# Forward bursts of batches 1 to 7 further apart, inverse bursts later, and the second layer of tile 2 as a direct product

## The chip, the cores and the metric

The kernel runs on one core of a Trainium2 chip. The metric is the time of one execution on the device, in microseconds (us). "Before" stands for the kernel as it was, "after" for the kernel with the change. The engines are called PE (TensorE's matmuls), PEld (its weight loads), DVE (VectorE), ACT (ScalarE), POOL (GpSimd) and SP (SyncE, which here only issues DMAs). L468 is line 468 of the kernel before.

## The reference

The input x has 8 batches of 3008 rows and 256 columns. Each column is filtered along its batch's rows in the frequency domain, and the result goes, row by row, through two dense layers with a Gelu between them.

```python
X = np.fft.rfft(x, axis=1)                       # x: 8 x 3008 x 256
y = np.fft.irfft(X * (filt_r + 1j * filt_i), n=3008, axis=1)
h = y.reshape(24064, 256) @ w_in                 # w_in: 256 x 2048
g = 0.5 * h * (1.0 + erf(h / sqrt(2)))
out = g @ w_out                                  # w_out: 2048 x 256
```

## The kernel before

**The filter.** 3008 is 47 x 64, and the transform is done as matmuls in stages. For batches 1 to 7 the stages are these. `fold` adds and subtracts halves of x on DVE, in place (L107, L108). `s1` (L430) multiplies by the first table; its result a_sb is stored to a DRAM tile R1 by SP (L439) and read back with another layout as b_sb by `r1` (L445). `s2` (L457) is the forward burst: 32 small matmuls into four PSUM banks. `s2_out` (L468) multiplies one of these four banks by the filter on DVE. On every second call it also combines the real and imaginary parts of a pair, by L471 and L472. `s3` (L485) is the inverse burst of the same unit: 32 small matmuls that read p, the result of `s2_out`. ACT copies it to v_sb, SP stores that to a DRAM tile R2 (L495), and `r2` (L503) reads it back as d_sb. `s4` (L512) finishes the inverse transform with four matmuls a call, and ACT or DVE writes the result into a ring y_sb. Each batch has three units u = 0, 1, 2 of `s2`, `s2_out`, `s3`, and b_sb has two buffers, so that the third `r1` follows the first unit's burst. Batch 0 goes another way, ahead of the main loop.

**The layers.** The 24064 rows are 47 tiles of 512. `mm1` (L637) makes one sixteenth of a tile's hidden layer by two matmuls of 512 columns (four where the tile wraps around the ring), and ACT applies Gelu (L640) into g_sb. The second layer of a tile is done, for all tiles but tile 0, by `mm2_seven` (L709): the 2 x 2 block product is made by seven products instead of eight, each in 16 matmuls of 128 columns, so 112 in all. It needs sums of quarters of g_sb, made on DVE by `sums_1` (L678, four calls a tile), `sums_2` (L684, two) and `sums_3` (L691, two). DVE also evacuates the products from PSUM and adds them up in eight operations a tile (L724 to L738). The products use two PSUM banks of the kind `o` in turn, a new one from products 0, 1, 3 and 5 on: L724 frees the first, L726 and L729 the second, L731 to L735 the third, the two of L738 the last. Tile 0 is done directly, by `mm2_first` (L650): 64 matmuls of 256 columns, and two copies from PSUM on DVE.

**The order.** Nothing is ordered by the machine. The main loop goes over slots s; slot s belongs to tile t = s // 16 and place jc = s % 16. In each slot the kernel first issues what a table `at` holds for this slot, then a sixteenth of the second layer of tile t - 1, then a sixteenth of the first layer of tile t:

```python
for f, a in at.pop(s, ()):
    f(*a)
...
if t - 1 in seven:
    ...
    m.mm2_seven(t - 1, n(jc), n(jc + 1))
```

So every engine's queue is in this order, and each engine works through its queue without passing anything by. The table is filled by hand-written formulas. `first(b)`, called `hi`, is the first slot of the tile in which batch b's rows begin: 80, 176, 272, 368, 464, 560 and 656 for batches 1 to 7. `sums_1` of a tile stand at places 12, 13 and 15 of its own tile and 1 of the next, `sums_2` at 0 and 1 of the next, `sums_3` at 5 and 8. `s1` of batches 3 to 6 stands at `hi - 94` to `hi - 83`, the first two `r1` at `hi - 80`. The slots of `s2` are the table `s2` in the code, and `s2_out`, `s3`, the third `r1`, the first `r2` (after[b]) and the loads of the next batch's x (`load_next`, on POOL, behind a small copy that waits for p) hang on them. `s4` is placed backwards from the slot in which its rows are needed, and goes out of the way of slots that are marked busy, which are those around bursts.

PSUM has three banks of the kind `h`, two `o` and three `f`. `s2` and `s3` take one `h` and three `f`; `s1` and `s4` use `f` too.

Of the kernel before, what the change touches and what calls it, by code (L numbers as in the profile page):

```python
# [10 lines left out]
ALU = mybir.AluOpType  # L11
# [11 lines left out]
TCH = 512  # L23
# [8 lines left out]
class _Mix:  # L32
# [428 lines left out]
    def s2_out(self, b, u, m, d):  # L461

        if d == 0:
            self.st[b, "p", 2 * u + m] = self.pp.tile([128, 2, 2, 2, 256], BF16, tag="p12", name="p12")
        w, a, v = self.st[b, "p", 2 * u + m], m ^ d, self.nc.vector.tensor_tensor
        ps = self.st[b, "ps2"][m][d].rearrange("p (r c) -> p r c", r=2)
        f = self.Fu[:, :, a, 2 * u + m, :]
        v(out=w[:, a], in0=ps.unsqueeze(2).to_broadcast([128, 2, 2, 256]),  # L468
          in1=f.unsqueeze(1).to_broadcast([128, 2, 2, 256]), op=ALU.mult)
        if d:  # L470
            v(out=w[:, :, 0, 0], in0=w[:, :, 0, 0], in1=w[:, :, 1, 1], op=ALU.subtract)  # L471
            v(out=w[:, :, 0, 1], in0=w[:, :, 0, 1], in1=w[:, :, 1, 0], op=ALU.add)  # L472

    def s3(self, b, u):

# [163 lines left out]
            o += n  # L639
        nc.scalar.activation(out=self.st["g", t][:, jc, :], in_=ps, func=AF.Gelu)  # L640

    def mm2_first(self, lo, hi):

        nc = self.nc
        for n in range(lo, hi):
            jc, q = (n // 2, n % 2) if n < 32 else (n % 16, n // 16)
            if n < 2:
                self.st["o2", q] = self.bank("ps_o", "o").rearrange("p (a b) -> p a b", a=2)
            ps = self.st["o2", q % 2]
            nc.tensor.matmul(ps[:, q // 2, :], lhsT=self.st["g", 0][:, jc, q * 128:q * 128 + 128],  # L650
                             rhs=self.w_out_sb[:, jc, :], start=(jc == 0), stop=(jc == 15))
            if q > 1 and jc == 15:
                ost = self.po.tile([128, 2, 256], FP32, tag="ost", name="ost")
                nc.vector.tensor_copy(out=ost, in_=ps)
                for a in range(2):
                    self.put_rows((q - 2 + 2 * a) * 128, ost[:, a], nc.sync)

    def weight_sums(self):

# [33 lines left out]
    def mm2_seven(self, t, lo, hi):  # L693

        nc, v = self.nc, self.nc.vector.tensor_tensor
        a11, a12, s2, a22 = self.quarters(t)
        w = self.w_out_sb.rearrange("p (i k) (n o) -> p k n i o", k=2, n=2)
        q = self.w_sums
        s31, s4 = self.st["s", t], self.st.get(("s4", t))
        ops = ((a11, w[:, 0, 0]), (a12, w[:, 1, 0]), (s2, q[:, 1]), (s31[:, :, 0], q[:, 2]),  # L700
               (s31[:, :, 1], q[:, 0]), (a22, q[:, 3]), (s4, w[:, 1, 1]))
        last = t == self.B * self.S // TCH - 1
        for n in range(lo, hi):
            m, sub, i = n // 16, n // 8 % 2, n % 8
            if n % 16 == 0 and (m == 0 or m % 2 == 1) or last and m > 4 and i == 0:
                self.st["o"] = self.bank("ps_o", "h" if n > 80 else "o").rearrange("p (m s o) -> p m s o", m=2, s=2)
            ps = self.st["o"]
            a, b = ops[m]
            nc.tensor.matmul(ps[:, (m + 1) % 2, sub, :], lhsT=a[:, i, 128 * sub:128 * sub + 128], rhs=b[:, i],  # L709
                             start=i == 0, stop=i == 7)  # L710
            if last and m > 4 and i == 7:
                self.finish(t, m, sub, ps)
            if n % 16 != 15 or m % 2 or last and m > 4:
                continue
            p0, p1 = ps[:, 0], ps[:, 1]
            if m == 0:
                self.st["t"] = self.po.tile([128, 2, 2, 128], FP32, tag="ost", name="t_sb")
                self.st["c"] = [None, None]
            if m in (2, 4):
                self.st["c"][m // 4] = self.po.tile([128, 2, 256], FP32, tag="ost", name="ost")  # L720
            t1, t3 = self.st["t"][:, 0], self.st["t"][:, 1]
            c = lambda h, k: self.st["c"][h][:, :, 128 * k:128 * k + 128]
            if m == 0:
                nc.vector.tensor_copy(out=t1, in_=p1)  # L724
            elif m == 2:
                v(out=c(0, 0), in0=t1, in1=p0, op=ALU.add)  # L726
                if last:
                    self.store(t, 0, 0, nc.sync)
                v(out=t1, in0=t1, in1=p1, op=ALU.add)  # L729
            elif m == 4:  # L730
                v(out=t3, in0=t1, in1=p0, op=ALU.subtract)  # L731
                v(out=c(1, 1), in0=t3, in1=p1, op=ALU.add)
                if last:
                    self.store(t, 1, 1, nc.scalar)
                v(out=t1, in0=t1, in1=p1, op=ALU.add)  # L735
            else:
                for h, tt, p in ((1, t3, p0), (0, t1, p1)):
                    v(out=c(h, 1 - h), in0=tt, in1=p, op=ALU.add)  # L738
                    for sub in range(2):
                        self.put_rows(t * TCH + 256 * h + 128 * sub, self.st["c"][h][:, sub],  # L740
                                      nc.gpsimd if t > 1 or h > sub else nc.sync)

    def put_rows(self, r0, tile_, eng):

# [33 lines left out]
def kernel(  # L778
# [9 lines left out]
    m = _Mix(ctx, tc, x, filt_r, filt_i, moe_w_in, moe_w_out, out)  # L788
    nc, B, S = tc.nc, m.B, m.S
    NT = B * S // TCH  # L790
    ctx.enter_context(tc.manual_schedule())

    g = m.small
# [112 lines left out]
    def put(slot, f, *a):  # L906
        at.setdefault(slot, []).append((f, a))

    def first(b):
        return (b * S // TCH) * 16  # L910

    busy, crowd, after = set(), set(), {}
    for b in range(1, B):
        hi = first(b)
        e = 4 * (b == B - 1)
        s1, n1, r1 = (4, 2.75, 16) if b == 1 else (hi - 87, 3.7, hi - 73) if b == 2 else (hi - 94 - e, 3.7, hi - 80 - e)
        s2 = (33, 45, 57) if b == 1 else (hi - 64 - 2 * e + (b == 2), hi - 48 - 3 * e + e // 4, hi - 32 - 3 * e)
        busy.update(range(s1 - 1, s1 + int(3 * n1) + 2))
        for c in range(4):
            slot = s1 + int(c * n1 + (b == 1 and c in (1, 2)))  # L920
            put((0, 1, 5, 8)[c] if b == 1 else (67, 69, 86, 94)[c] if b == 2 else s1 - 28 + e + 6 * c, m.fold, b, c)
            put(slot, m.s1, b, c)
        for u in range(3):
            put(r1 if u < 2 else s2[0] + 1, m.r1, b, u)
            put(s2[u], m.s2, b, u)
            for i in range(4):
                put(s2[u] + ((0, 2, 5, 6)[i] if b == u == 1 else 2 * i + (b == 2 and u == 0)), m.s2_out, b, u, i // 2, i % 2)
            s3 = s2[u] + (9 if b == 1 and u != 1 else 10)
            put(s3, m.s3, b, u)
            put(s3 + 1, m.s3_out, b, u, 1)  # L930
            busy.update(range(s2[u] - 1, s2[u] + 5), range(s3 - 1, s3 + 2))
        after[b] = s3 + (5 if b > 1 else 4)
        crowd.update(range(s2[0], after[b]), range(s1 + 66, s1 + 94))
        if b + 1 < B:
            for i, (u, o, p) in enumerate(((0, 5, 1), (0, 7, 1), (1, 1, 2), (1, 5, 3), (1, 7, 3), (2, 1, 4), (2, 5, 5), (2, 7, 5))):
                put(s2[u] + o, m.load_next, b, p, i // 2, i % 2)
# [34 lines left out]
    put(1, m.load_filters_again, nc.gpsimd, 0, 2)  # L971
    put(18, m.load_filters_again, nc.sync, 2, 4)
    put(20, m.weight_sums)
    seven = range(1, NT)
    for t in seven:
        for i, s in enumerate((12, 13, 15, 16 if t == S // TCH - 1 else 17)):
            put(16 * t + s, m.sums_1, t, 2 * i)
# [5 lines left out]
    for s in range((NT + 1) * 16):  # L983
        t, jc = s // 16, s % 16
        for f, a in at.pop(s, ()):
            f(*a)
        pace = lambda i: max(16 * (i - 6) // 10, 0) if t == late else i
        if t - 1 in seven:
            n = lambda i: (14 * i if i < 6 else 84 + 28 * (i - 6) // 10) if t == late else 7 * i
            m.mm2_seven(t - 1, n(jc), n(jc + 1))  # L990
        elif t < 2:
            n = lambda i: max(4 * i - 40, 0) if i < 16 else min(24 + 8 * (i - 16) // 3, 64)
            m.mm2_first(n(s), n(s + 1))
        for i in range(pace(jc), pace(jc + 1)) if t < NT else ():
            m.mm1(t, i)
    assert not at
# [30 lines left out]
```

## Time and profile before

| What | Value |
|---|---|
| Time, median of 3 runs (lowest to highest) | 751.08 us (750.72 to 751.89) |
| Time of the profiled execution | 750.39 us |
| Its span | 748.6 us |
| PE busy | 730.8 us, 9261 matmuls |
| DVE busy | 616.9 us, 1120 instructions |
| ACT busy | 575.1 us, 1048 instructions |
| POOL busy | 288.2 us, 544 instructions |
| Granted clock of PE | 1.00 |
| Sums and evacuations a tile on DVE | 4 of L678 at 687 ns, 2 of L684 at 707, 2 of L691 at 693, 8 evacuations at 413 to 421 |
| A unit on DVE | 4 of L468 at 1217 ns, 2 each of L471 and L472 at 432 and 436 |

The span goes from the first to the last instruction of the profiled execution; the time of the execution has 1.8 us around it. An instruction on DVE shows its whole duration, and the next may start a little before its end, so lengths of a queue are counted from start to start. Ends of matmuls are modelled, so PE's own waits are also read from start to start. A line of a timeline gives start and duration in us, engine, line and operation, what it writes and reads, how many instructions are merged, and in brackets the idle time before it and what ended that.

### The profile page before, as it was taken

To read this page: it belongs to the slowest core of one execution; us is meant where nothing else is said; L and a number is where in the kernel's file an instruction comes from. 1 tells how busy PE (TensorE), PEld (TensorE's weight loads), DVE (VectorE), ACT (ScalarE), POOL (GpSimd) and SP (SyncE) were. 2 spreads that over 40 slices of the span, in tenths; PEclk is the share of its full clock that TensorE was granted. 3 is DMA by queue.
4 is the path that set the end of the run, shared out by engine and by line. 5 is a ranking of instruction groups with operands and counts; after the bars stand their busy time and mean duration, and the time that the engine had idled before them with its cause. 6 is when DMAs were issued, how large, how long until landed. Compare 5 with 4: busy or idle time off the path is not lost.

```text
span 748.6 us, 22400 instructions
## 1 busy us (share of the span) xinstructions
PE 730.8 (98%) x9261; PEld 508.9 (68%) x9261; DVE 616.9 (82%) x1120; ACT 575.1 (77%) x1048; POOL 288.2 (39%) x544
## 2 busy tenths in 40 slices
PE   8999999999999999999999999999999999999997
PEld 4856666666777667666677666666767766777776
DVE  8977998899887998789977989769997898676566
ACT  6987777677887788878887777877878787777773
POOL 7893446666122552234431355114631122112121
PEclk9999999999999999999999999999999999999999
DMA  9996542745345552546535455355444433301011
GB/s 154 213 193 185 125 109 86 212 90 123 86 121 177 117 119 82 142 148 134 112 103 162 111 126 131 90 158 129 117 108 118 153 91 99 117 31 58 29 57 58
DMA packets 81353, 89.31 MB, mean 119 GB/s; under 512 B 13171, under 2 KB 60659, under 8 KB 81251
## 3 DMA queue, kind: packets, MB, share of 16 engines
q0 software_dynamic: 22352, 39.76, 23.1%
q1 hardware_dynamic: 58483, 47.93, 22.8%
q8 instruction: 72, 1.18, 0.7%
q14 instruction: 30, 0.25, 0.1%
q10 hardware_dynamic: 416, 0.20, 0.1%
HBM read 55.57 MB, written 48.23 MB: 139 GB/s over the span
## 4 chain that ended last, share of the span: by engine, by line
PE 77%; DVE 15%; DMA 3%; POOL 2%; issue 2%; ACT 0%; DVEq 0%; POOLq 0%; SPq 0%
PE ps_h L637 35%; PE ps_o L709 33%; DVE p L468 5%; DMA x_sb<-in_x_dram 3%; PE ps_s L512 2%; PE ps_s L430 2%; DVE s_sb L678 2%; POOL out_dram L756 1%; PE ps_s L485 1%; DVE p L472 1%; PE ps_s L457 1%; DVE g_sb L684 1%; PE ps_o L650 1%; DVE s_sb L691 1%; DVE x_sb L108 1%
## 5 line engine op out<-in xcount | busy, mean ns | idle before, releaser
L640 ACT ACTIVATE g_sb<-ps_h 128x512 f16<-128x512 f32 x752 | 447.9, 603 | 146.1 <-PE ps_h L637 142.5
L637 PE MATMUL ps_h<-y_sb,w_in_sb 128*128 128x512 bf16 (+3 forms) x1600 | 445.3, 366 | 0.2 <-DVE a_sb L328 0.2
L756 POOL DMA_DIRECT2D out_dram<-ost x228 | 129.4, 574 | 389.3 <-DVE ost L738 359.4
L709 PEld LDWEIGHTS <-g_sb 128*128 128x128 f16 x2944 | 193.9, 98 | 90.1 <-issue 13.5
L709 PEld LDWEIGHTS <-s_sb 128*128 128x128 f16 x2208 | 147.8, 98 | 56.7 <-issue 3.7
L709 PE MATMUL ps_o<-w_sums,g_sb 128*128 128x128 f16 x1472 | 127.5, 219 | 4.7 <-DVE t_sb L729 3.5
L637 PEld LDWEIGHTS <-w_in_sb 128*128 128x128 bf16 x1600 | 125.0, 98 | 8.5 <-issue 1.1
L709 PE MATMUL ps_o<-w_sums,s_sb 128*128 128x128 f16 x1472 | 126.2, 219 | 0.1
L709 PE MATMUL ps_o<-w_out_sb,g_sb 128*128 128x128 f16 x1472 | 119.4, 219 | 2.1 <-DVE ost L738 2.1
L678 DVE TENSOR_TENSOR s_sb<-g_sb 128x1024 f16<-128x1024 f16 x184 | 120.3, 687 | 0.8 <-ACT g_sb L640 0.8
L468 DVE TENSOR_TENSOR p<-ps_s,F 128x1024 bf16<-128x1024 f32 x84 | 102.1, 1217 | 3.5 <-PE ps_s L457 1.8
L99 POOL DMA_DIRECT2D x_sb<-in_x_dram x156 | 79.0, 513 | 2.4 <-DMA x_sb<-in_x_dram 0.8
L684 DVE TENSOR_TENSOR g_sb<-s_sb,g_sb 128x1024 f16<-128x1024 f16 x92 | 65.0, 707 | 1.6
L709 PE MATMUL ps_o<-w_out_sb,s_sb 128*128 128x128 f16 x736 | 63.9, 219 | 0.0
L691 DVE TENSOR_TENSOR s_sb<-g_sb 128x1024 f16<-128x1024 f16 x92 | 63.8, 693 | 0.0
L731 DVE TENSOR_TENSOR t_sb<-t_sb,ps_o 128x256 f32<-128x256 f32 x46 | 19.3, 419 | 40.9 <-PE ps_o L709 39.7
L326 ACT ACTIVATE v_sb<-ps_s 128x512 bf16<-128x512 f32 x83 | 45.5, 608 | 6.3 <-PE ps_s L485 5.7
L326 ACT ACTIVATE y_sb<-ps_s 128x376 bf16<-128x376 f32 x94 | 46.6, 496 | 4.6 <-PE ps_s L512 4.6
L512 PEld LDWEIGHTS <-d_sb 96*128 96x128 bf16 x448 | 31.2, 97 | 27.2 <-issue 2.2
L738 DVE TENSOR_TENSOR ost<-t_sb,ps_o 128x256 f32<-128x256 f32 x90 | 33.7, 415 | 18.1 <-PE ps_o L709 18.1
L328 DVE CAST a_sb<-ps_s 128x512 bf16<-128x512 f32 x54 | 34.7, 684 | 12.7 <-PE ps_s L430 12.4
L726 DVE TENSOR_TENSOR ost<-t_sb,ps_o 128x256 f32<-128x256 f32 x46 | 19.1, 416 | 24.7 <-PE ps_o L709 24.1
(156 smaller groups left out, 556.7 us busy)
## 6 DMA issues: line engine op xcount, KB each, us to landing
out_dram<-ost POOLq DMA_DIRECT2D x126, 128.0 KB, 2.7
b_sb<-R SPq DMA_DIRECT2D x21, 512.0 KB, 5.2
R<-v_sb SPq DMA_DIRECT2D x84, 128.0 KB, 2.6
d_sb<-R SPq DMA_DIRECT2D x56, 192.0 KB, 3.3
R<-a_sb SPq DMA_DIRECT2D x108, 96.0 KB, 2.2
x_sb<-in_x_dram POOLq DMA_DIRECT2D x48, 94.0 KB, 2.7
x_sb<-in_x_dram POOLq DMA_DIRECT2D x48, 48.0 KB, 2.7
x_sb<-in_x_dram POOLq DMA_DIRECT2D x12, 188.0 KB, 5.1
```

Of the source, the lines that this page charges most:

```text
L99: self.nc.gpsimd.dma_start(out=xt[64 * v + to:64 * v + to + m, h, 4 * c:4 * c + 4 * n, :], in_=xv[h][at:at + m, w:w + 4 * n, :])
L326: self.nc.scalar.activation(out=out, in_=in_, func=AF.Copy, scale=1.0 if scale is None else scale)
L328: self.nc.vector.tensor_copy(out=out, in_=in_)
L468: v(out=w[:, a], in0=ps.unsqueeze(2).to_broadcast([128, 2, 2, 256]), in1=f.unsqueeze(1).to_broadcast([128, 2, 2, 256]), op=ALU.mult)
L512: nc.tensor.matmul(ps[:, 94 * i:94 * i + 94], lhsT=d[:, (grp % 2) * 4 + i, 128 * half:128 * half + 128], rhs=self.T4a[:, 4 * grp + i, 0:2 ...
L637: nc.tensor.matmul(ps[:, o:o + n], lhsT=w[:, dc], rhs=self.ring[:, dc, off:off + n], start=(dc == 0), stop=(dc == 1))
L640: nc.scalar.activation(out=self.st["g", t][:, jc, :], in_=ps, func=AF.Gelu)
L678: self.nc.vector.tensor_tensor(out=self.st["s", t][:, i:i + 2], in0=a, in1=b, op=ALU.subtract)
L684: self.nc.vector.tensor_tensor(out=a21[:, k], in0=self.st["s", t][:, k, 0], in1=a22[:, k], op=ALU.add)
L691: self.nc.vector.tensor_tensor(out=self.st["s4", t][:, k], in0=a12[:, k], in1=s2[:, k], op=ALU.subtract)
L709: nc.tensor.matmul(ps[:, (m + 1) % 2, sub, :], lhsT=a[:, i, 128 * sub:128 * sub + 128], rhs=b[:, i], start=i == 0, stop=i == 7)
L756: eng.dma_start(out=out, in_=tile_[lo - r0:lo - r0 + n])
```

## The change

Five things are changed.

- The slots of `s2`. Batch 1: 28, 43, 58 instead of 33, 45, 57. Batch 2 (hi = 176): 113, 129, 145 instead of 113, 128, 144. Batches 3 to 6: `hi - 72`, `hi - 53`, `hi - 34` instead of `hi - 64`, `hi - 48`, `hi - 32`, which puts them at places 8, 11 and 14 of a tile instead of 0, 0 and 0. Batch 7: 580, 596, 612 instead of 584, 597, 612, at places 4, 4 and 4.
- The two operations L471 and L472 leave `s2_out` for a step of their own, `s2_sum`, one slot after the second and fourth `s2_out`.
- `s3` follows `s2` after 13 slots (12 in batch 1) instead of 10 (9 for units 0 and 2 of batch 1). The first `r2`, `load_next`, the third `r1` and the places of `s4` follow from it.
- Tile 2's second layer is made like tile 0's, by 64 matmuls of 256 columns, four a slot in slots 48 to 63, with two copies by DVE; its sums are left out. Its rows are stored by POOL's queue, as before.
- In tile 1 the rows of half 0 are stored by POOL's queue instead of SP's.

```diff
--- before.py
+++ after.py
@@ -467,9 +467,12 @@
         f = self.Fu[:, :, a, 2 * u + m, :]
         v(out=w[:, a], in0=ps.unsqueeze(2).to_broadcast([128, 2, 2, 256]),
           in1=f.unsqueeze(1).to_broadcast([128, 2, 2, 256]), op=ALU.mult)
-        if d:
-            v(out=w[:, :, 0, 0], in0=w[:, :, 0, 0], in1=w[:, :, 1, 1], op=ALU.subtract)
-            v(out=w[:, :, 0, 1], in0=w[:, :, 0, 1], in1=w[:, :, 1, 0], op=ALU.add)
+
+    def s2_sum(self, b, p):
+
+        w, v = self.st[b, "p", p], self.nc.vector.tensor_tensor
+        v(out=w[:, :, 0, 0], in0=w[:, :, 0, 0], in1=w[:, :, 1, 1], op=ALU.subtract)
+        v(out=w[:, :, 0, 1], in0=w[:, :, 0, 1], in1=w[:, :, 1, 0], op=ALU.add)
 
     def s3(self, b, u):
 
@@ -639,21 +642,25 @@
             o += n
         nc.scalar.activation(out=self.st["g", t][:, jc, :], in_=ps, func=AF.Gelu)
 
-    def mm2_first(self, lo, hi):
+    def mm2_first(self, t, lo, hi):
 
         nc = self.nc
         for n in range(lo, hi):
-            jc, q = (n // 2, n % 2) if n < 32 else (n % 16, n // 16)
-            if n < 2:
-                self.st["o2", q] = self.bank("ps_o", "o").rearrange("p (a b) -> p a b", a=2)
-            ps = self.st["o2", q % 2]
-            nc.tensor.matmul(ps[:, q // 2, :], lhsT=self.st["g", 0][:, jc, q * 128:q * 128 + 128],
+            if t:
+                q, jc = n // 16, n % 16
+            else:
+                jc, q = (n // 2, n % 2) if n < 32 else (n % 16, n // 16)
+            if jc == 0 and (q % 2 == 0 if t else q < 2):
+                self.st["o2", q // 2 if t else q] = self.bank("ps_o", "o").rearrange("p (a b) -> p a b", a=2)
+            ps, a = (self.st["o2", q // 2], q % 2) if t else (self.st["o2", q % 2], q // 2)
+            nc.tensor.matmul(ps[:, a, :], lhsT=self.st["g", t][:, jc, q * 128:q * 128 + 128],
                              rhs=self.w_out_sb[:, jc, :], start=(jc == 0), stop=(jc == 15))
-            if q > 1 and jc == 15:
+            if jc == 15 and (q % 2 if t else q > 1):
                 ost = self.po.tile([128, 2, 256], FP32, tag="ost", name="ost")
                 nc.vector.tensor_copy(out=ost, in_=ps)
-                for a in range(2):
-                    self.put_rows((q - 2 + 2 * a) * 128, ost[:, a], nc.sync)
+                for i in range(2):
+                    self.put_rows(t * TCH + ((q - 1 + i) if t else (q - 2 + 2 * i)) * 128, ost[:, i],
+                                  nc.gpsimd if t else nc.sync)
 
     def weight_sums(self):
 
@@ -738,7 +745,7 @@
                     v(out=c(h, 1 - h), in0=tt, in1=p, op=ALU.add)
                     for sub in range(2):
                         self.put_rows(t * TCH + 256 * h + 128 * sub, self.st["c"][h][:, sub],
-                                      nc.gpsimd if t > 1 or h > sub else nc.sync)
+                                      nc.gpsimd if t > 1 or h * sub == 0 else nc.sync)
 
     def put_rows(self, r0, tile_, eng):
 
@@ -914,7 +921,7 @@
         hi = first(b)
         e = 4 * (b == B - 1)
         s1, n1, r1 = (4, 2.75, 16) if b == 1 else (hi - 87, 3.7, hi - 73) if b == 2 else (hi - 94 - e, 3.7, hi - 80 - e)
-        s2 = (33, 45, 57) if b == 1 else (hi - 64 - 2 * e + (b == 2), hi - 48 - 3 * e + e // 4, hi - 32 - 3 * e)
+        s2 = (28, 43, 58) if b == 1 else (hi - 63, hi - 47, hi - 31) if b == 2 else (hi - 72 - e, hi - 53 - 7 * e // 4, hi - 34 - 5 * e // 2)
         busy.update(range(s1 - 1, s1 + int(3 * n1) + 2))
         for c in range(4):
             slot = s1 + int(c * n1 + (b == 1 and c in (1, 2)))
@@ -924,12 +931,14 @@
             put(r1 if u < 2 else s2[0] + 1, m.r1, b, u)
             put(s2[u], m.s2, b, u)
             for i in range(4):
-                put(s2[u] + ((0, 2, 5, 6)[i] if b == u == 1 else 2 * i + (b == 2 and u == 0)), m.s2_out, b, u, i // 2, i % 2)
-            s3 = s2[u] + (9 if b == 1 and u != 1 else 10)
+                put(s2[u] + 2 * i + (b == 2 and u == 0), m.s2_out, b, u, i // 2, i % 2)
+            for i in range(2):
+                put(s2[u] + 3 + 4 * i + (b == 2 and u == 0), m.s2_sum, b, 2 * u + i)
+            s3 = s2[u] + (12 if b == 1 else 13)
             put(s3, m.s3, b, u)
             put(s3 + 1, m.s3_out, b, u, 1)
             busy.update(range(s2[u] - 1, s2[u] + 5), range(s3 - 1, s3 + 2))
-        after[b] = s3 + (5 if b > 1 else 4)
+        after[b] = s3 + (5 if 1 < b < B - 1 else 4)
         crowd.update(range(s2[0], after[b]), range(s1 + 66, s1 + 94))
         if b + 1 < B:
             for i, (u, o, p) in enumerate(((0, 5, 1), (0, 7, 1), (1, 1, 2), (1, 5, 3), (1, 7, 3), (2, 1, 4), (2, 5, 5), (2, 7, 5))):
@@ -971,7 +980,8 @@
     put(1, m.load_filters_again, nc.gpsimd, 0, 2)
     put(18, m.load_filters_again, nc.sync, 2, 4)
     put(20, m.weight_sums)
-    seven = range(1, NT)
+    plain = (0, 2)
+    seven = [t for t in range(NT) if t not in plain]
     for t in seven:
         for i, s in enumerate((12, 13, 15, 16 if t == S // TCH - 1 else 17)):
             put(16 * t + s, m.sums_1, t, 2 * i)
@@ -990,7 +1000,9 @@
             m.mm2_seven(t - 1, n(jc), n(jc + 1))
         elif t < 2:
             n = lambda i: max(4 * i - 40, 0) if i < 16 else min(24 + 8 * (i - 16) // 3, 64)
-            m.mm2_first(n(s), n(s + 1))
+            m.mm2_first(0, n(s), n(s + 1))
+        elif t - 1 in plain:
+            m.mm2_first(t - 1, 4 * jc, 4 * jc + 4)
         for i in range(pace(jc), pace(jc + 1)) if t < NT else ():
             m.mm1(t, i)
     assert not at
```

## The prediction

> **What bounds the kernel now.** The page first: TensorE (PE) is busy nearly throughout, at full granted clock, and VectorE (DVE) is the next busiest.
>
> ```profile
> PE 730.8 (98%) x9261; PEld 508.9 (68%) x9261; DVE 616.9 (82%) x1120; ACT 575.1 (77%) x1048; POOL 288.2 (39%) x544
> ```
>
> A busy PE isn't a PE at its pace, so I took the starts of its matmuls. They follow each other by 0.216 us at 512 columns, 0.109 at 256 (L650) and 0.056 at 128 (L709). A slot with two of L637 and seven of L709 thus lasts 0.823. Wherever a start comes later than that, PE waited. Over the span these delays come to some 18 us after 50 us, and nearly all end with DVE, as the waits of PE say (total, times, longest):
>
> ```profile
> PE ps_o L709 <- DVE t_sb L729: 3.5, 5, 0.7
> PE ps_o L709 <- DVE ost L738: 2.1, 3, 0.7
> PE ps_s L512 <- DVE p L468: 1.7, 1, 1.7
> PE ps_s L485 <- DVE p L468: 0.6, 1, 0.6
> ```
>
> These are idle times from modelled ends; start to start each is 0.1 to 0.2 longer, and the short ones are missing. So PE sets the time, plus what DVE's single queue is late by. The change moves DVE's bursts; the question is what stands behind a burst in that queue. Two places have a short fuse. The second PSUM bank `o` of a tile's products is asked for again at matmul 16 of the next tile (third matmul of its slot 2), and is freed by L738, queued at the end of slot 15. And the sums of L684, queued in slots 0 and 1, are read at matmuls 32 and 36 (slots 4 and 5).
>
> Batch 7's unit 0 shows such a queue. Its forward burst starts on PE at 590.89, in slot 584, slot 8 of its tile:
>
> ```profile
> 591.44 1.22 DVE L468 TENSOR_TENSOR p<-ps_s,F 128x1024 bf16<-128x1024 f32 x1 [0.87 <-PE ps_s L457]
> 592.58 0.68 DVE L691 TENSOR_TENSOR s_sb<-g_sb 128x1024 f16<-128x1024 f16 x1
> 593.18 1.22 DVE L468 TENSOR_TENSOR p<-ps_s,F 128x1024 bf16<-128x1024 f32 x1
> 594.43 0.42 DVE L471 TENSOR_TENSOR p<-p 128x512 bf16<-128x512 bf16 x1
> ...
> 595.11 0.41 DVE L731 TENSOR_TENSOR t_sb<-t_sb,ps_o 128x256 f32<-128x256 f32 x1
> ...
> 596.22 1.22 DVE L468 TENSOR_TENSOR p<-ps_s,F 128x1024 bf16<-128x1024 f32 x1
> 597.36 1.28 DVE L678 TENSOR_TENSOR s_sb<-g_sb 128x1024 f16<-128x1024 f16 x2
> 598.56 1.21 DVE L468 TENSOR_TENSOR p<-ps_s,F 128x1024 bf16<-128x1024 f32 x1
> ...
> 600.48 0.69 DVE L678 TENSOR_TENSOR s_sb<-g_sb 128x1024 f16<-128x1024 f16 x1
> 601.09 0.74 DVE L738 TENSOR_TENSOR ost<-t_sb,ps_o 128x256 f32<-128x256 f32 x2
> ```
>
> DVE never rests for 10.4 us, and L738 comes last, at 601.84, 10.95 after the burst's start. On PE:
>
> ```profile
> 600.12 0.81 PE L485 MATMUL ps_s<-p,U 32*64 32x256 bf16 x32
> 600.87 0.28 PE L709 MATMUL ps_o<-w_out_sb,g_sb 128*128 128x128 f16 x2
> 601.88 0.44 PE L709 MATMUL ps_o<-w_out_sb,g_sb 128*128 128x128 f16 x5 [0.73 <-DVE ost L738]
> ```
>
> PE waits 0.9 there, though an inverse burst and two bursts of s4 had delayed it before. From start to start in DVE's queue: L468 1.14, L471 with L472 0.69, each L678, L684 or L691 0.60 to 0.70, the three evacuations from L731 1.11, L738 twice 0.67. In batches 3 to 6 the units now start in slot 0 of a tile, after L738, so this queue isn't met there.
>
> **The change, part by part.** Sums are made on the profiled execution (750.39, span 748.6 and 1.8 around it); the median of the three runs is 0.69 higher, so the difference is put on that.
>
> *Batches 3 to 6: new waits.* Unit 0 moves to slot 8 of a tile (slot 200 in batch 3), unit 1 to slot 11, unit 2 to slot 14. Unit 0 then has just the queue above: the same operations in the same order (L471 and L472, a slot later, still lie before L731, and before the last L678). L738 ends 10.95 after the burst's start. PE is there earlier than in batch 7: burst 0.56, ten slots 8.23, one s4 0.17, two matmuls 0.11, 9.07 in all, as the inverse burst now lies three slots further on. Wait: 10.99 - 9.07 = 1.92. Unit 1: DVE starts 0.55 after the burst and does three L468, one pair, three sums, three evacuations and L738: 3.42 + 0.69 + 1.80 + 1.11 + 0.67, so it ends at 8.24; PE is there after 0.56 + 7 x 0.823 + 0.11 = 6.43. Wait 1.85. Behind L738 the second L684 comes after another 3.06 (L684, L468, L678, L684), at 11.30; PE, restarted at 8.28, reads it 2.41 later: wait 0.65. Unit 2: L738 is early, but the second L684 (6.71 against 6.55) and L724 (8.19 against 7.85) are late by 0.2 and 0.3; I take 0.4 (0 to 0.7). New: 4.8 a batch.
>
> *Batches 3 to 6: waits removed.* The inverse bursts now wait for L471 and L472 (0.26, 0.26 and 0.09 over a burst that doesn't wait); they come three slots later and the pair one slot later, 1.6 us more, and DVE has caught up by then. Twice L724 (0.17) and once L729 (0.87) hold a bank. All go: 1.8. Net 4.8 - 1.8 = 3.0 a batch, 12.0 for four. Bounds: with unit 0's wait and half of unit 1's 1.1 net a batch (+4.5), with another microsecond +16.
>
> *The earlier read of b_sb, batches 3 to 7.* Loads r1 stay at their slot; the burst comes 8 slots after them instead of 12 to 16: 6.6 us with two or three s4, 7.0. SyncE issues the load when the stores of R1 have landed:
>
> ```profile
> 579.37 1.42 SPq L439 DMA_DIRECT2D R<-a_sb  x3
> 583.96 0.81 SPq L445 DMA_DIRECT2D b_sb<-R  x2
> ```
>
> Here that is 3.3 after the slot's start (580.62), and the sixteenth increment of the first load's semaphore comes at 587.95, 7.3 after it. In batches 5 and 6 it is 6.8 and 7.2. In 3 and 4, where a load of d_sb ran ahead of it, 9.6 and 8.3; that load moves to slot 183, ahead of two of the stores, as it lies in batch 7. So PE waits 0 to 0.4; I take 0.3 each, 1.5 in all, bounds 0 (all as in batch 5) and 12.5 (batch 3's landing each time). A wait here delays PE and the burst's own work on DVE alike, so it takes nothing off the other waits. Behind the third load, which waits for the burst, SyncE now holds r2 of the batch before, read 13 slots later: 0.
>
> One rule by itself: the Trainium skill, "DMA: Bandwidth & Descriptors" (Specifications), gives 0.6 us to the first byte and about 358 GB/s for a core from HBM; by that 512 KB would be there after 2.1 us (an estimate), no burst would wait, and the sum would be 1.5 lower. The trace's loads took 3.5 to 7.9 us.
>
> *Batch 7.* Units go to slot 4 of their tiles, where unit 2 stands now without a wait. The 0.15 and 0.89 at unit 0 go: -1.0 (bounds -1.0 and 0.5).
>
> *Batch 2.* Units 1 and 2 move by one slot, inverse bursts by three or four: waits at L471/L472 (0.36, 0.26, 0.26), L724 (0.17 twice) and L729 (0.87) go, -2.1. One stays: at 151.56 an s4 waits 1.85 for its bank, freed by an L468 at 153.4 that is late because POOL's table work slows L472 and L691 beside it (1.20 and 1.30 us, 0.44 and 0.69 on the mean). That s4 moves a slot earlier, the L468 doesn't: +0.9, and 0.2 at the next. Net -1.0 (-3 to 1).
>
> *Batch 1 and tile 2.* PE loses 1.26 + 0.75 + 0.19 + 0.43 at units and twice 0.75 to 0.90 at L738: 4.3. Tile 2 drops eight sums (4.9 us of DVE) and eight evacuations for two copies of 0.69, so unit 1 finds an empty queue. Unit 0 now stands among the sums of tile 1: counted as above, L684 and L724 are late by 0.8, 0.6 and 0.35. Unit 2 does the same to tile 3: 0.9. Net -1.6. Direct matmuls cost PE 64 x 0.109 - 112 x 0.056 = 0.7. The first s4 gets its d_sb 8 slots after r2 instead of 12: 10.7 us after the inverse burst's start, where the chain of v_sb, R and d_sb took 13.0 amid other transfers that now lie ahead of it; 0.3 (0 to 2). Two moves of rows from SyncE to POOL (0.57 an issue) delay only x_sb loads, needed 20 slots later: 0. Part: -0.6.
>
> *What moves along.* SyncE's stores of v_sb go three or four slots later, the first r2 of a batch one to four; s4 still has 13 slots or more after the last inverse burst in batches 2 to 7, over 10 us, so 0 outside batch 1. POOL's gates and x loads come earlier, into the 359 us that POOL idles before out_dram: 0. Behind each wait of PE lies all of its queue, and ACT's Gelus with it (77% busy, so ACT recovers).
>
> Sum: 12.0 + 1.5 - 1.0 - 1.0 - 0.6 = 10.9, so 751.08 + 10.9 = 762.0.
>
> **Rivals.** *Faster:* DVE has room before the old bursts; from 222.5 on it is busy 4.69 of 6.80 and 4.23 of 6.90 us:
>
> ```profile
> 222.50:229.30 6.80, 6.80 (x79) 4.91 (x77) 4.69 (x10) 4.96 (x9) 2.84 (x5) 1.00 0.86 265
> 229.30:236.20 6.90, 6.90 (x85) 4.89 (x81) 4.23 (x9) 5.34 (x10) 0.00 (x0) 1.00 0.41 126
> ```
>
> Unit 0 goes into it. If PE can reach matmul 16 without L738's bank, or L738 ends within 9.07, the gains alone are left: 4 x -1.8 - 1.0 - 1.0 - 0.6 = -9.8, 741.3. Against it is the order of the queue, met in batch 7. Decided by whether PE waits for L738 in slot 210. *Half:* only unit 0 collides (1.9 against 1.8 a batch) and b_sb is as taken: 750 to 753. *Transfer-bound:* every b_sb lands as in batch 3, 9.6 after its slot: another 2.3 x 5, 773. *Not as said:* the direct tile could keep PE waiting for DVE's copies; they free a bank 16 slots before its next use, so no.
>
> **How the numbers follow.** Forecast 0.78, faster rival 0.09, half 0.07 (in it 0.03 within 0.2%, about what a measurement of this kernel tells from no change), transfer-bound 0.06. Slower: 0.88. The range takes the bound of the net wait in batches 3 to 6 (down to +4.5, 754.5) and on the other side 16 instead of 12 with 2 more for b_sb: 768.
>
> **What would show it.** Right: PE waits on L738 of about 1.9 us in slots 210 and 226 of batch 3 and their like every 96 slots, waits on L684 behind the second, none at L485 for L471/L472, 64 matmuls at L650's line more in tile 2, and a chain with more DVE. Wrong: no wait on L738 in batches 3 to 6, or long ones at L457 for b_sb.

## The result, and the profile after

The kernel after takes 760.66 us in the median of 4 runs (760.20 to 760.86), the kernel before 750.92 beside it. The ratio is 1.0126, with an interval of 1.0109 to 1.0144: 1.3% slower. The profiled execution took 760.49 (span 758.6, granted clock 1.00), 10.1 more than that of before. In after the lines have moved: L709 is now L716, L738 is L745, L684 is L691, L724 is L731, L729 is L736, L637 is L640, L471 and L472 are L474 and L475, L503 is L506; L445, L457 and L468 stand where they stood.

The page of after, part 1:

```profile
PE 728.0 (96%) x9213; PEld 507.0 (67%) x9213; DVE 605.3 (80%) x1104; ACT 574.2 (76%) x1050; POOL 291.0 (38%) x547
```

DVE has 11.6 us less to do than before and PE 2.8, and still the time is longer. So it isn't the work of PE or DVE that grew (POOL has 2.8 us more, at 38% busy); the waits of PE did. The waits of PE in after (total, times, longest):

```profile
PE ps_o L716 <- DVE ost L745: 14.7, 9, 1.8
PE ps_o L716 <- DVE g_sb L691: 5.3, 11, 0.9
PE ps_s L515 <- DVE p L468: 1.6, 1, 1.6
...
PE ps_o L716 <- DVE t_sb L731: 0.9, 5, 0.2
```

L745 alone has gone from 2.1 us in 3 waits (as L738) to 14.7 in 9: two in each of batches 3 to 6 and one in batch 2. No wait on b_sb stands in the list. Here is unit 0 of batch 3 on DVE, the queue that the prediction counted through (start, duration, engine, line and operation; in brackets the idle time before it and what ended that):

```profile
228.62 1.23 DVE L468 TENSOR_TENSOR p<-ps_s,F 128x1024 bf16<-128x1024 f32 x1 [0.75 <-PE ps_s L457]
...
235.75 1.22 DVE L468 TENSOR_TENSOR p<-ps_s,F 128x1024 bf16<-128x1024 f32 x1
237.00 0.43 DVE L474 TENSOR_TENSOR p<-p 128x512 bf16<-128x512 bf16 x1
237.34 0.42 DVE L475 TENSOR_TENSOR p<-p 128x512 bf16<-128x512 bf16 x1
237.68 0.69 DVE L685 TENSOR_TENSOR s_sb<-g_sb 128x1024 f16<-128x1024 f16 x1
238.28 0.75 DVE L745 TENSOR_TENSOR ost<-t_sb,ps_o 128x256 f32<-128x256 f32 x2
```

The burst started on PE at 228.08; L745 ends at 239.03, 10.95 later, and nowhere from 228.62 on did DVE rest. PE in the same place:

```profile
237.05 0.28 PE L716 MATMUL ps_o<-w_out_sb,g_sb 128*128 128x128 f16 x2
239.08 0.45 PE L716 MATMUL ps_o<-w_out_sb,g_sb 128*128 128x128 f16 x5 [1.76 <-DVE ost L745]
```

Two matmuls of slot 210 are done, the third needs the bank: 239.08 less 237.05 less twice 0.056 is 1.92 from start to start.

Where the time went, by the start of the first-layer matmul of a slot, after minus before:

| Stretch | Change of the difference, us | Forecast |
|---|---|---|
| up to slot 16 | +0.35 | not foreseen |
| slots 16 to 88 (batch 1, tile 2) | -0.94 | -0.6 |
| slots 88 to 192 (batch 2) | -0.85 | -1.0 |
| slots 192 to 560 (batches 3 to 6) | +12.92 | +12.0 and 4 x 0.3 for b_sb |
| slots 560 to 640 (batch 7) | -1.06 | -1.0 and 0.3 for b_sb |
| slot 640 to the end | -0.38 | not foreseen |

Together 10.04, the difference of the spans. The first row need not come from the change: after and the runs below with the phases back and with another phase do the same work up to slot 16, and reach it at 52.60, 52.25 and 52.28.

### The profile page after: what moved, and what is told of

The parts are those of the page before. It is cut to its first block, busy times and chain, and to the rows that moved or that the text cites. A ratio compares the mean times of both kernels' runs of the same rounds, so it can differ in the third digit from the quotient of the medians.

```text
span 758.6 us, 22296 instructions
## 1 busy us (share of the span) xinstructions
PE 728.0 (96%) x9213; PEld 507.0 (67%) x9213; DVE 605.3 (80%) x1104; ACT 574.2 (76%) x1050; POOL 291.0 (38%) x547
## 3 DMA queue, kind: packets, MB, share of 16 engines
q8 instruction: 72, 1.18, 0.6%
## 4 chain that ended last, share of the span: by engine, by line
PE 70%; DVE 22%; DMA 3%; issue 2%; POOL 2%; ACT 0%; DVEq 0%; POOLq 0%
PE ps_h L640 32%; PE ps_o L716 29%; DVE p L468 8%; DVE s_sb L685 4%; DMA x_sb<-in_x_dram 2%; PE ps_s L515 2%; DVE g_sb L691 2%; PE ps_s L430 2%; PE ps_o L656 2%; PE ps_s L488 2%; DVE ost L745 1%; PE ps_s L457 1%; POOL F L141 1%; DVE p L475 1%; DVE p L474 1%
## 5 line engine op out<-in xcount | busy, mean ns | idle before, releaser
L640 PE MATMUL ps_h<-y_sb,w_in_sb 128*128 128x512 bf16 (+3 forms) x1600 | 445.3, 366 | 0.2 <-DVE a_sb L328 0.2
L716 PEld LDWEIGHTS <-g_sb 128*128 128x128 f16 x2880 | 189.9, 98 | 105.3 <-DVE ost L745 16.3
L763 POOL DMA_DIRECT2D out_dram<-ost x231 | 131.5, 575 | 332.6 <-DVE ost L745 323.1
L716 PEld LDWEIGHTS <-s_sb 128*128 128x128 f16 x2160 | 144.0, 98 | 55.6 <-issue 8.0
L716 PE MATMUL ps_o<-w_sums,g_sb 128*128 128x128 f16 x1440 | 126.5, 219 | 5.7 <-DVE g_sb L691 5.3
L640 PEld LDWEIGHTS <-w_in_sb 128*128 128x128 bf16 x1600 | 125.8, 98 | 9.2 <-issue 2.6
L716 PE MATMUL ps_o<-w_out_sb,g_sb 128*128 128x128 f16 x1440 | 117.7, 219 | 14.7 <-DVE ost L745 14.7
L716 PE MATMUL ps_o<-w_sums,s_sb 128*128 128x128 f16 x1440 | 123.5, 219 | 0.9 <-DVE t_sb L731 0.9
L468 DVE TENSOR_TENSOR p<-ps_s,F 128x1024 bf16<-128x1024 f32 x84 | 102.4, 1220 | 27.2 <-PE ps_s L457 27.2
L685 DVE TENSOR_TENSOR s_sb<-g_sb 128x1024 f16<-128x1024 f16 x180 | 118.3, 686 | 0.6 <-ACT g_sb L643 0.6
L691 DVE TENSOR_TENSOR g_sb<-s_sb,g_sb 128x1024 f16<-128x1024 f16 x90 | 64.0, 712 | 1.5
L698 DVE TENSOR_TENSOR s_sb<-g_sb 128x1024 f16<-128x1024 f16 x90 | 62.5, 695 | 0.0
L716 PE MATMUL ps_o<-w_out_sb,s_sb 128*128 128x128 f16 x720 | 62.5, 219 | 0.0
L146 POOL COPY gate<-p 1x1 bf16<-1x1 bf16 x48 | 16.4, 342 | 116.4 <-DVE p L468 116.3
L738 DVE TENSOR_TENSOR t_sb<-t_sb,ps_o 128x256 f32<-128x256 f32 x45 | 18.8, 418 | 43.9 <-PE ps_o L716 43.9
L745 DVE TENSOR_TENSOR ost<-t_sb,ps_o 128x256 f32<-128x256 f32 x88 | 33.0, 417 | 10.3 <-PE ps_o L716 10.3
```

What stands on the lines that cost most here:

```text
L640: nc.tensor.matmul(ps[:, o:o + n], lhsT=w[:, dc], rhs=self.ring[:, dc, off:off + n], start=(dc == 0), stop=(dc == 1))
L685: self.nc.vector.tensor_tensor(out=self.st["s", t][:, i:i + 2], in0=a, in1=b, op=ALU.subtract)
L691: self.nc.vector.tensor_tensor(out=a21[:, k], in0=self.st["s", t][:, k, 0], in1=a22[:, k], op=ALU.add)
L698: self.nc.vector.tensor_tensor(out=self.st["s4", t][:, k], in0=a12[:, k], in1=s2[:, k], op=ALU.subtract)
L763: eng.dma_start(out=out, in_=tile_[lo - r0:lo - r0 + n])
```

## The experiments

"The queue theory" says that PE's waits are the queue that stands behind a burst in DVE's order, counted from the places in a tile. "Phase" is the place of a burst in its tile of 16 slots. Waits are read from start to start.

**Phases back in after.** Units of batches 3 to 6 at their old places, the rest of the change kept, but for the inverse bursts there, which follow after 12 slots instead of 13.

```diff
-... else (hi - 72 - e, hi - 53 - 7 * e // 4, hi - 34 - 5 * e // 2)
+... else (hi - 76, hi - 60, hi - 44) if b == B - 1 else (hi - 64, hi - 48, hi - 32)
-            s3 = s2[u] + (12 if b == 1 else 13)
+            s3 = s2[u] + (12 if b == 1 or 2 < b < B - 1 else 13)
```

> The kernel after, with the units of batches 3 to 6 alone back at place 0 of their tiles (hi - 64, - 48, - 32); the inverse bursts there come 12 slots after the forward ones (13 leaves s4 no room). Theory of the queue: what is lost is that L745 and L691 (L738 and L684 of before) stand behind a unit's work in DVE's queue, and the place of the burst in its tile decides it. The 5.1 us of waits in each of batches 3 to 6 fall to 0.4 to 0.9 (the bank freed by L736), so 743 to 746 us, faster than before too. Rival of the distance: units that live longer (inverse bursts later, p and PSUM held longer) cost the time, wherever they start. Then it stays within 2 us of 760.7.

Measured: 742.26 us (741.89 to 743.25), ratio to before 0.9884 (0.9870 to 0.9899), 0.7 below the range expected. From the list of PE's waits there:

```profile
PE ps_o L716 <- DVE t_sb L736: 2.3, 4, 0.7
...
PE ps_o L716 <- DVE ost L745: 0.7, 1, 0.7
```

All eight waits on L745 in batches 3 to 6 are gone; one on L736 is left in each (0.57, 0.57, 0.91, 0.91), and the single L745 is batch 2's. So the new phases of four batches cost 18.4 us (760.66 - 742.26; in the traces 17.5 of it lies between slots 192 and 560), and what is left of the change is 1.2% faster than before. The fall in L745 is what the queue theory says; the rival had no place for it.

**The phases alone, in before.** The other side: only the slots of `s2` in batches 3 to 6 are moved; no `s2_sum`, `s3` after 10 slots, tile 2 by seven products.

```diff
-... else (hi - 64 - 2 * e + (b == 2), hi - 48 - 3 * e + e // 4, hi - 32 - 3 * e)
+... else (hi - 72, hi - 53, hi - 34) if 2 < b < B - 1 else (hi - 64 - 2 * e + (b == 2), ...)
```

> The kernel before, with the slots of the units of batches 3 to 6 alone as in after (hi - 72, - 53, - 34); inverse bursts 10 slots later as before, L471 and L472 where they were, tile 2 by seven products. Theory of the queue: the waits come with the places alone. The inverse burst now lies inside unit 0's wait and fills 0.8 of it, so about 1.1 at L738 for unit 0 and 1.8 for unit 1, 1 to 1.5 for L471/L472 and L684 behind; 4.3 a batch instead of 1.8, 759 to 763 us. Rival of the distance: 750 to 753 us.

Measured: 767.97 us (767.16 to 768.35), ratio 1.0223 (1.0208 to 1.0238): 5 us beyond what was expected. The waits on L738 were there (0.90 and 2.03 a batch), but a line came first that after doesn't have:

```profile
PE ps_s L457 <- DMA b_sb<-R: 3.9, 4, 1.1
```

Unit 0's burst waited 1.20, 0.90, 1.12 and 0.94 for its load in batches 3 to 6, though the burst stands eight slots behind `r1` as in after. Together that is 4.2 us. Why was open here, and is settled below; with these waits gone the same work takes 764.27, still 1.3 over the range expected. Part of that is behind unit 1, where 1.8 was expected for the 2.03.

**Tile 2 by seven products in after.**

```diff
-    plain = (0, 2)
+    plain = (0,)
```

> The kernel after, with tile 2 by seven products again. Theory of the queue: DVE gets eight sums and six evacuations more into slots 44 to 63, beside units 1 and 2 of batch 1; waits of about 1.4 at L745 in slot 50, 0.6 at L691 in 53, 1.2 at L745 in 66 and 0.4 more at L691 in 69 come, 0.7 of PE's matmuls go: 762.5 to 764.5 us. Rival: the direct tile costs its 0.7 of PE and brings nothing: 759.9 us.

Measured: 766.71 us (766.17 to 767.54), ratio 1.0207 (1.0190 to 1.0225).

```profile
PE ps_o L716 <- DVE ost L745: 17.4, 11, 1.8
PE ps_o L716 <- DVE g_sb L691: 6.2, 12, 1.2
PE ps_s L457 <- DMA b_sb<-R: 2.6, 3, 1.0
```

Two waits on L745 come back in batch 1 (1.83 and 1.17), with 0.66 and 0.37 more on L691: 4.0, less the 0.7 that the 64 wider matmuls cost, is 3.3, within what was expected. The rest is again waits on b_sb, of 0.68, 1.11 and 1.05 in batches 3, 6 and 7 and 0.2 in batch 5, batches that the edit doesn't touch.

**The third L685 of a tile one slot later, in after.** It then stands behind L745 in the queue instead of ahead of it.

```diff
-        for i, s in enumerate((12, 13, 15, ...)):
+        for i, s in enumerate((12, 13, 16, ...)):
```

> The kernel after, with the third sum of each tile (L685 at place 15) put one slot later, so behind L745 instead of ahead of it. Theory of the queue: L745 comes 0.6 earlier in the queue, so the waits at L745 in batches 3 to 6 go from 1.92 and 1.90 to about 1.3 each, and the next wait for L691 grows by the same 0.6 (0.64 to 1.2); the sum is near 0, 759.5 to 761.5 us. Rival: the bank is held by something other than the queue (the bursts on PE, ACT, transfers): the waits at L745 stay at 1.9.

Measured: 759.67 us (759.16 to 760.62), ratio 1.0116 (1.0101 to 1.0131). The waits on L745 in batches 3 to 6 are 1.32 and 1.29 instead of 1.92 and 1.90, one L685 (0.60) shorter; the one on L691 behind is 1.24 instead of 0.64 (in batches 5 and 6 1.07 instead of 0.47). The same queue, in another order: what it saved at one bank it gave back at the next reader.

```profile
PE ps_o L716 <- DVE ost L745: 9.2, 8, 1.2
PE ps_o L716 <- DVE g_sb L691: 8.9, 14, 1.1
```

**Another phase in each batch, in after.**

```diff
-... (hi - 72 - e, hi - 53 - 7 * e // 4, hi - 34 - 5 * e // 2)
+... (hi - (71, 70, 69, 67)[b - 3], hi - 53, hi - 34)    # batches 3 to 6
```

> The kernel after, with unit 0's forward burst of batches 3, 4, 5 and 6 at hi - 71, -70, -69 and -67 (places 9, 10, 11 and 13 of its tile instead of 8); units 1 and 2 as in after. Queue theory (what stands behind the burst in DVE's order before L745 sets the wait): a wait of unit 0 on L745 of about 1.4 us in batch 3 and 1.45 in batch 4 (from there with a wait on L691 of about 1.1 behind it), 1.9 to 2.1 in batch 5, where unit 0 has the place that unit 1 has, and none on L745 in batch 6 but about 1.2 on L691; unit 1's waits 1.9, 1.9, 1.7 and 1.4. In all 759 to 762. Rival (it is the distance of 16 to 19 slots between units or the load on DVE in general, not the place in the tile): a wait on L745 of 1.8 to 2.0 in all four batches.

Measured: 760.50 us, one run.

```profile
PE ps_o L716 <- DVE ost L745: 10.7, 8, 1.7
```

Unit 0's wait on L745 was 1.22 in batch 3 and 1.16 in batch 4 (there with 1.14 on L691), 1.90 in batch 5, none in batch 6, where L691 held PE for 1.31; unit 1's were 1.90, 1.90, 1.91 and 1.16. The place sets which wait it is, as the theory says; the distance between the units, 14 to 18 slots here, doesn't. Each is within 0.3 of what was expected. Of the places 8 to 11 and 13 none is free: a burst's eight operations on DVE meet L745 or the second L691. In batch 6, with its units 14 slots apart, unit 1's burst also waited 1.24 for ACT's copies out of PSUM.

**Tile 2 direct, alone, in before.**

```diff
-    seven = range(1, NT)
+    plain = (0, 2)
+    seven = [t for t in range(NT) if t not in plain]
...
+        elif t - 1 in plain:
+            m.mm2_first(t - 1, 4 * jc, 4 * jc + 4)
```

> The kernel before with only tile 2's second layer made direct; every slot of s2, s2_sum and s3 as before. Theory: DVE's queue of batch 1 gets shorter by tile 2's sums and evacuations, so the waits of 0.75 to 0.9 us on L738 in slots 50 and 66 and part of that at unit 1 go, 1.8 to 2.5 together, against 0.7 us that 64 matmuls of 256 columns cost PE over 112 of 128: 749 to 750, 1 to 2 us faster than before. Rival (the waits of batch 1 come from the bursts' slots, which stay): 751.5 to 752, the price of the matmuls alone.

Measured: 748.59 us (10 runs, 747.19 to 751.30), ratio 0.9971 (0.9962 to 0.9980). The waits on L738 in slots 50 and 66 are gone (0.75 and 0.90); the one that is left (L738 is L742 here) is batch 7's:

```profile
PE ps_o L713 <- DVE ost L742: 0.7, 1, 0.7
```

Those at the inverse bursts of units 1 and 2 are gone as well (1.3 together), hence a little more than expected. The emptier queue of batch 1 is worth more than the wider matmuls cost, with the bursts at their old places here as at their new ones in the run with tile 2 by seven products.

**PE's code moved, the work kept.** What differs between after (no wait on b_sb) and the runs with such waits? Not the transfers of b_sb: the same stores and loads, the same distance to the burst. But the trace's list of DMA queues has one of kind "instruction", and in a stretch of the trace one can see whether it moved anything. In after, from the slot of `r1` of batch 3 to the landing of its first load (221.3 to 227.5):

```profile
q1 hardware_dynamic: 752, 1.08, 56.2%
q0 software_dynamic: 189, 0.44, 18.0%
```

Queue, kind, packets, MB, share: rows and loads only. The run with the phases alone, in the same stretch (222.4 to 230.5), has a third line:

```profile
q8 instruction: 1, 0.02, 0.7%
```

Over the whole execution of after this queue moves 72 packets, 1.18 MB: 16 KB each, some 10 us apart. Over 18,426 matmuls and weight loads that is 64 bytes an instruction, so it is PE's code. To test it, the ten matmuls of the first warm-up (whose product nobody reads) became more and narrower ones. That shifts the code behind them and costs little.

```diff
-m.warm_up(10)            # 10 matmuls of 512 columns
+m.warm_up(43, 120)       # in after
+m.warm_up(81, 64)        # in the kernel with the phases alone
+m.warm_up(58, 88)        # in after, a later run
```

> The kernel before with only the slots of s2 of batches 3 to 6 moved (the run with the phases alone, 767.97 us), and the first warm-up of PE as 81 matmuls of 64 columns instead of 10 of 512: 142 instructions more in PE's code, fetches some 6.5 us earlier against the work. In the run with the phases alone the fetches start 6.0, 4.9, 0.4 and 0.1 us after the slot of r1 in batches 3 to 6; shifted they come just before that slot or close to the burst (about 5.6 in batch 6). Theory (fetch): the waits on b_sb of 1.20, 0.90, 1.12 and 0.94 go in batches 3 to 5 to 0.3 or less, batch 6 keeps up to 1: 764 to 766. Rival (transfers' order): the same four waits, 767.5 to 768.5.

Measured: 764.27 us (763.97 to 765.80), ratio 1.0181 (1.0168 to 1.0194). All four waits on b_sb are gone, batch 6's too, and the run is 3.7 us faster than the same work with the code where it was.

> The kernel after, with the first warm-up of PE made of 43 matmuls of 120 columns instead of 10 of 512: about the same time on PE, but 33 matmuls (66 instructions) more in PE's code, so that every later fetch of PE's code (72 packets of 16 KB in the traces of before and after) should come some 3 us earlier against the work. In after these fetches start at 229.2, 322.2, 414.9, 509.2 and 599.1, each just after the first load of b_sb has landed; 3 us earlier each falls into the load. Theory (the waits on b_sb that the run with the phases alone showed and after doesn't come from such a fetch, which holds up the last sixteenth of a load by some 1.5 us): waits of 0.4 to 1.2 at s2 of unit 0 in most of batches 3 to 6, perhaps in batch 7, and 762.5 to 765.5. Rival (the transfers' own order decides, not the fetch): no wait on b_sb, 760.0 to 761.5.

Measured: 760.86 us (760.34 to 762.28), ratio 1.0135 (1.0121 to 1.0148). This run alone is inconclusive. The profiled execution, the longest of the four, had waits of 0.57 and 1.20 in batches 5 and 6; the fetches had not all come 3 us earlier (in batches 3 and 4 they started at 228.5 and 322.1, 0.7 and 0.1 earlier), and the median is hardly above that of after. In batch 7 a packet came in the load as well and made no wait. So one more, with just as many matmuls more as tile 2 has by seven products:

> The kernel after, with the first warm-up of PE as 58 matmuls of 88 columns instead of 10 of 512. That is 48 matmuls more in PE's code, just as many as tile 2 has more by seven products, so from tile 4 on PE's code lies as in the run with tile 2 by seven; the work stays that of after. Theory (fetches of PE's code that meet the stores of R1 or the load of b_sb cause that run's waits on b_sb of 0.68, 1.11 and 1.05 us in batches 3, 6 and 7): waits of 0.5 to 1.2 at s2 of unit 0 in these three batches, 762.5 to 764.5. Rival (those waits came with tile 2's work or the later times, not with the place of the code): no such waits, 760.0 to 761.5.

Measured: 764.45 us (763.87 to 765.51), ratio 1.0183 (1.0166 to 1.0200), with the work of after and 3.8 us slower than it. PE waited on b_sb in all five batches, the three expected and two more, 0.56, 0.93, 0.38, 0.84 and 0.63 (3.3 together):

```profile
PE ps_s L457 <- DMA b_sb<-R: 3.0, 5, 0.9
```

The other 0.8 us of its profiled execution arose in batch 1, in the same way: a load of the filter F, landed at 58.07 in after, landed here at 62.33, its sixteenth increment 1.5 us after the fifteenth, with a packet of PE's code at 60.25; and the first L468 of unit 0, which reads F, came 0.9 later after its slot's start.

Batch 3's burst in this run:

```profile
229.45 0.63 PE L457 MATMUL ps_s<-b_sb,T2p 64*32 64x256 bf16 x32 [0.49 <-DMA b_sb<-R]
```

Between the slot of `r1` and the landing of the first load, three profiled executions compare as follows (times after the slot's start, batches 3, 4, 5, 6, 7; a load has landed with the sixteenth increment of its semaphore):

| Kernel | Packet of PE's code in the stretch | Load issued | Sixteenth increment |
|---|---|---|---|
| before | in each | 2.1, 2.1, 3.0, 3.4, 3.3 | 9.6, 8.3, 6.8, 7.2, 7.3 |
| after | in none | 2.2, 2.2, 2.0, 2.0, 2.0 | 6.2, 6.2, 5.9, 5.9, 5.7 |
| after, code as with tile 2 by seven | in each | 2.1, 2.2, 3.2, 3.6, 3.3 | 7.3, 7.7, 6.8, 7.3, 7.2 |

The phases-alone kernel has a packet in all four stretches of batches 3 to 6, and with its code shifted in none. Seven of the profiled executions have bursts of unit 0 eight slots behind `r1` (after, the third L685 later, tile 2 by seven, the phases alone, and the three with code moved), 33 such bursts in batches 3 to 7. In 17 a packet lay between the slot's start and the landing, and 15 of these waited, 0.2 to 1.2 us; the two that didn't had their loads landed at 6.3 and 6.4. Of the 16 without a packet none waited. That the place of PE's code decides is shown by these runs. How it does so is read from the traces only, and not shown by a run: where the packet came during the load (batches 3 and 4 of the last row), the sixteenth increment came 1.3 and 1.2 us after the fifteenth, as if one of the sixteen parts of the load had been held up; where it came during the stores of R1, the load was issued 1.2 to 1.6 us later.

**A better version.** Bursts back where the queue behind them is short, tile 2 direct and `s2_sum` kept.

```diff
-        s2 = (28, 43, 58) if b == 1 else (hi - 63, hi - 47, hi - 31) if b == 2 else (hi - 72 - e, ...)
+        s2 = (26, 41, 56) if b == 1 else (114, 131, 146) if b == 2 else (hi - 76, hi - 60, hi - 44) if b == B - 1 else (hi - 62, hi - 47, hi - 32)
-            s3 = s2[u] + (12 if b == 1 else 13)
+            s3 = s2[u] + (12 if b < B - 1 else 13)
```

> The kernel after with bursts put where the queue behind them is free: units of batches 3 to 6 at hi - 62, -47, -32 (places 2, 1 and 0 of a tile), batch 1 at 26, 41, 56, batch 2 at 114, 131, 146, batch 7 as in after; inverse bursts 12 slots behind (13 in batch 7); direct tile 2 and s2_sum kept. From the run with the phases put back (742.26 us): its waits on L736 of 0.57, 0.57, 0.91 and 0.91 in batches 3 to 6 go, and so do the waits of batch 1 on L691 (1.01, 0.66, 0.94) and of batch 2 on L745 (0.88) for the most part; the s4 of batch 2 keeps 1.9 to 2.0. 738.5 to 741, faster than both kernels. Rival (the waits are moved, not removed: sums of tile 1 or L731 come late instead): 741.5 to 743.

Measured: 740.48 us (739.66 to 742.19), ratio to before 0.9862 (0.9839 to 0.9886), faster than both kernels. The waits on L736 didn't go, against the theory's part of the expectation:

```profile
PE ps_o L716 <- DVE g_sb L691: 2.7, 4, 1.2
PE ps_o L716 <- DVE t_sb L736: 2.3, 4, 0.7
```

So the total came into the expected range by another sum than the one given. These waits are 0.56, 0.56, 0.90 and 0.90, as with the phases back: in front of L736 stands the `fold` of the next batch (L107, L108), which I hadn't counted there. The gain came from batches 1 and 2: the s4 of batch 2 waits 1.01 instead of 2.02, its L745 0.45 instead of 0.88, and the wait of 0.94 on L691 in batch 1 is gone.

## Why the prediction was right, and where it was not

*Batches 3 to 6, new waits: right.* Unit 0 was forecast at 1.92 and is 1.92; unit 1 at 1.85 and is 1.90; L691 behind it at 0.65 and is 0.64, 0.64, 0.47 and 0.47. Unit 2 was mis-sized: 0.4 taken, 0.62 to 0.79 measured (L691 0.27 to 0.44, L731 0.35). New waits come to 5.1 a batch for a forecast 4.8; this is where the 0.9 comes from by which these batches cost more than forecast. That this is the queue behind the burst, and not the load on DVE in general, is shown by the phases back, the third sum and the other places.

*Batches 3 to 6, removed: right.* 1.8 a batch forecast; 5.1 less the net 3.2 (12.92 / 4) leaves 1.9 measured. With the phases back, the L736 wait is there again, so that its absence in after is the new phase's doing, not that of `s2_sum`.

*The earlier read of b_sb: wrong in size and in part of what its rows showed.* 1.5 forecast, 0 measured in after, 3.3 with the same work and its code elsewhere. The step that failed is the reading of the landings in before's batches 5 to 7: I took 6.8 to 7.3 for the landing as such, "so PE waits 0 to 0.4". By the table above each of the five landings had a packet of PE's code in it. The run with tile 2 direct alone in before settles what was the packet's part: it has the filter in the order of before, and no packet in any of the five stretches. There the loads landed 7.8, 10.4, 6.5, 6.4 and 5.7 after their slots, for 9.6, 8.3, 6.8, 7.2 and 7.3. So in batches 5 to 7 the packet made up to 1.6 of the landing. The long landings of batches 3 and 4 come without a packet too, and the trace has loads of d_sb issued ahead of them there as well; that part of the reading stands. In after, with neither, the load lands 5.7 to 6.2 after its slot, ahead of every burst. Taking 64 matmuls for 112 in tile 2 (and so 96 instructions less) is a part of the change that moved the code; the prediction had no term for that, and that the cost of the earlier read came out as 0 and not as 3.3 is luck. The transfer-bound rival, 2.3 us more for each of five loads, was not met in any run: the longest wait was 1.20.

*Batch 7: right.* -1.0 forecast, -1.06 measured.

*Batch 2: the sum right, two of its steps wrong.* The s4's wait was to grow by 0.9; it is 1.80 for 1.85, as the L468 that frees its bank came earlier as well (152.21 for 153.4). In its place PE waits 0.89 on L745 in slot 162. In before the same stretch of DVE's queue (unit 2, then `fold`, then three sums) made PE wait 0.87 on L729; I counted that as removed, and it only moved on to the next bank.

*Batch 1 and tile 2: right in sign, small in size.* -0.6 forecast, -0.94 measured. The waits behind units 0 and 2 (1.01, 0.66, 0.35; 0.94) are near the 0.8, 0.6, 0.35 and 0.9 forecast. The 0.3 taken for the first s4, which gets its d_sb sooner after r2, was 0: no wait on d_sb stands in the list of after.

*Rivals.* The faster one (741.3) was to be decided by a wait on L738 in slot 210. It is there at 1.92, so that rival fell. Its figure, the gains without the new waits, is near what the run with the phases back took, 742.26. The half case fell with unit 1, and in after the direct tile kept PE waiting for nothing.

The forecast of 762.0 is 1.3 above the median. The sum behind it was 10.9 and the measured one 10.0: b_sb was 1.5 too high, batches 3 to 6 were 0.9 too low, the small terms nearly cancel.

## What to carry to other kernels

Where every engine works through a fixed order, cost a moved burst by counting what stands behind it in the queue of the engine that serves it, up to the operation that frees the next bank, against what the bound engine does meanwhile. A stall that goes from one bank should be looked for at the next. And before a transfer's spread in a trace is explained by other transfers, look whether a code fetch lies in it: adding or dropping instructions far away can then change the time.

## What the runs showed of the hardware

PE's code comes in 72 packets of 16 KB through the DMA queues while the kernel runs, one every 10 us or so, each lasting 0.9 to 1.9 us in the traces of before and after. The Trainium skill, "Trainium Architecture — The Big Picture" (The software stack), says that instructions have 64 bytes, with which 1.18 MB over 18,426 agrees. The same section has the streams moved to the engines' memory when the program is loaded; the trace of after shows the 72 packets spread over its execution, from 14.8 to 752.3 us, and the measurement decides.

On its own a shift of the code by 96 instructions, without a change of the filter or the layers, made after 3.8 us slower (760.66 to 764.45), and one by 142 made the phases-alone kernel 3.7 us faster, about as much as many an edit is worth here.
